# One-bank operations for the channel mix, the DFT pair and the output projection of a gated recurrence with long convolution

## The chip, the cores and the metric

The kernel runs on one core of a Trainium2 chip. The metric is the device time of one execution in microseconds. The engines are TensorE (PE, with its weight loads shown apart as PEld), VectorE (DVE), ScalarE (ACT), GpSimd (POOL) and SyncE (SP), which issues the DMAs. PE writes only to PSUM, which has eight banks of 512 f32 values per partition; ACT and DVE carry results out of it ("evictions").

## The reference

Batch B = 4, sequence S = 6272 = 128 x 49, D = 256 channels.

```python
sig = 1.0 / (1.0 + np.exp(-f_logit))
f = lower_bound + (1.0 - lower_bound) * sig
i = 1.0 - f
for t in range(S):                 # the recurrence
    h = f[:, t] * h + i[:, t] * x[:, t]
    y[:, t] = h
...
proj = y @ w_proj                  # [B, S, 3 D] -> x1, x2, x3
X2 = np.fft.rfft(x2, n=S, axis=1)
H = np.fft.rfft(filter_fft, n=S, axis=0)
x2_conv = np.fft.irfft(X2 * H, n=S, axis=1)
out = (x1 * x2_conv * x3) @ w_out
```

## The kernel before, in words

The kernel works through the four batches, with the recurrence of the next batch spread over the current one. The transform of length 6272 is split as 128 (m) times 49 (q).

- **Recurrence** (`hgrn`): PE turns chunks of x and f_logit (`su`, line 374, f32, two row tiles of 64 rows), ACT or DVE makes the gate (`f`, lines 387 and 389), DVE scans (line 395) and writes the states as f16 into `HA`, channels on partitions, time along the row.
- **P** (`phase_p`, line 720), the channel mix to x2: for each of the 49 residues r, the stationary operand is a column of HA, every 49th element (`column`, line 716), and the moving one is `W2`, 256 columns; two matmuls (one for each half kh of the states' channels) accumulate. Four r fill two banks. The eviction `x2` (line 732) writes f16 into X2, one run of four for each output channel. P reads all states of the batch.
- **F1** (`phase_f1`, line 737), the DFT over m: eight matmuls of 128 columns for a unit of eight channel pairs, two banks, evicted as `A` (line 745). 16 units a batch, four at a time.
- **F2** (line 804), the DFT over q, two banks, then the product with the filter's spectrum: directly by DVE from PSUM (line 827), or by a copy to A and POOL (line 836).
- **I2** (line 842), the inverse over q: both halves o of the product, 16 matmuls of 98 columns into two banks, evicted as `Th` (line 851).
- **Gate** (`gate`): x1 and x3 by matmuls x13 (line 423, one bank each); their product z goes to `zt` (line 444 by DVE, line 453 by POOL).
- **Output** (`phase_o`, line 896): I1 (line 909), the inverse over m; DVE multiplies by z into `ys` (line 915, f32r, two buffers); proj (line 927) multiplies by w_out into two banks, evicted as `o` into a staging place, and SP stores it.

The copies carry the line of the helper `copy`: 289 and 291 for ACT, 294 and 296 for DVE. So a group is told by its output tile: X is x2, HA 128x1024 is A, HA 98x512 is the copy ahead of POOL's product, Th, osb or PP is o.

Nothing is scheduled at run time. Each step is declared with `op(kind, cost, fn, r, w, take, src)`: what it reads and writes as tokens, how many banks it takes, and for an eviction the operation that it empties. The text `ORDER` (line 126) then lists all operations in the order in which they are emitted. Three characters in base 64 hold one of them: its index, its engine, and its first bank (`Plan.order`, line 100). So the order on each engine, the engine of each eviction and every bank are written out. An operation of PE is of one of two kinds: those that use tiles of 64 rows (`ROWS`, line 65: su, F2, mini, I1, FF2, last) and those that use all rows.

```python
word = a * 4096 + b * 64 + c
yield word // 64, self.ENGINES[word // 8 % 8], word % 8
```

At the start the filter is transformed (f2, FF1, FF2), its spectrum is written to DRAM, and each unit loads its part again (`Hu`). `pads` zeroes the gaps of X2 between the runs.

Of the kernel before, what the change touches and what calls it, by code (L numbers as in the profile page):

```python
# [25 lines left out]
Q = 49  # L26
# [27 lines left out]
def q_of(r):  # L54

    return (18 * r) % Q
# [6 lines left out]
class Plan:  # L63
# [63 lines left out]
    "AAYAPYA0gA4gA5YACIADIAQIAWIA1AAiQAdQA8gAkQAbQBAgBIgAcQAeQAgQA2QAhSAfSA9YA6SApUAjUA+UAmWBEgBQgBMgBBYATYAzIARAASAA7CA3"  # L127
    "IAUIBCWA/MBFIBDGAsQAoQAtQBJYBKQAxSAlSBGSArWAXABHKBYgDogBUgBggBcgBkgDrgDpgDsgEDgDqgD3gAnWAZWBRABSUBZAAaOAEgD4gEbgEEgB"
    "NYBOSAvWBLAEPgEQgAYYBVYBTMBPKABIAqWBaWAyUBbGBWUBdIBhYAuSBiSBjKBeWBlYBXEBfGDtAAwQBmQEFAAVYBnIBoWBpOBqQBrIBsYBxSBvWByK"
    "BwODuYBtQBuIB4SB6WD5AB5KB7OB0UB1EAFYBzYB8YD6YDvQCBSCCCDzUDwIDxID0EB/WCAGCDYEGYD1MCKSB9QCLKCEWD7UCFOEdAB+AD8ECISCJCCR"  # L130
    "QD/WCPSERACSACQCD9MCNUEHQCOECUSEAOEBOCYWEcgEzgEngEogEIIEJIE0gELUE9gCVCCMYCTYESYCZGE1ACaSCbCCfWCgGEMMENMChQCiIETSEpAE"
    "eYCcYCjYEqYCdWEXUCeGCoQEYEEUKEVKCkWEZMCpAClGEfSE/ACvQCqUEjWEgKCwIEhKCrEEkGCxQErUCyIElOCtSFHgAGgFJAEvQEsEEtME+gCWgFIg"
    "FRgCuCAHgFSgFbgC4WEwAExIEKYE2YCsYAIYAJYAKYCzYE3SFAYC6UC5GE4CC7EFKYC8YAMYC0WE5KE6QC1GC/UE7IDBSFTADAMDCCE8IFBWC9UFESFC"
    "GC+EFDOFFCCHgFcgFlgB3gFmgFvgFwgDIQDJADKUDLEDEWDFGALIEWYAOYDDYDMYFUYDyYFLQFOUFGKFPEDPSFMIFNIDQCFdAFQMDaWDNSDOCDbGFeYA"
    "NYFVQFYUFZEFnAFWIFXIDRSJSWJTXFfQJUGDSCJVHFxAFaMJXWFiSFgIJZOFhIFjCDUUDVEFkKFoYFpWDhQEmYDTYEiYEuYFyYD2YEOYECYEaYD+YFsU"
    "DfSFqGFrODiADYQFtEDgCDZAFuMFzWDkSF0GF2QEyADdUCGgB2gC3gDeEDlCC2gMXgDHgG2gCXgMWgF5gCmgMigDXgCngF+gDcYDjYJWYMYAF6YF7YMZ"
    "YGkgDmgMvgDngMjgDGgDWgMugGtgG/gF1OJYWJcXF3IJeHF4IGMQGCUGISGJCJauGNIGDMGQQGGWGHOGUSGYUGVKGRAGOQGKWGPIMkAGZEGLGGEUGFEG"
    "ASGSWGWUGBKGTGJdSJhTJiWJfqGXEGaUGbEJjLJkuGcQGdAGgSGhKGeWJmUJnVGfGF8QJoMJpNGlSGuWGiUF9AGpqGyGG3QGjMJrXJsTG5AGnqGwuJbY"
    "GqYJqYJtHHIUJwXJxQGxYGmYJuDGzYGoYGvYJyHJzoGrSG7oHJEHAWG0UGsCG1EHOSHPCJ1RJ2QHKUHEuG4YJvYG6YG8YHBYMlYHFYJ3JHCuHLEJ6XHM"
    "SJ7RJ8PJ4oJ9pHNCG9UHTWG+EHSgHDYHQSJ/QHGUKARHbgHkgHtgHXGKBAHRKMwAHVuKCpHcSHHEHlWHnGKERHeqHgqH2UHWYHdYKFWKJSKGBHfYHUYH"  # L140
# [24 lines left out]
    "kUXFAXGIXSQafCXaSdeAXbCUlMUqOXgUXYWXMSXhEXTIXWUXNKXXMXZGXOWXPGdqAUmSXiUUnKXUWXeQXQSXVOXfIXjEd2AXKWXRCXLGXcUXdEUogUjg"
    "UzSUuQdfYUrWUvIU0KdrYXIYXJYd3YUsGXmUacYXnMXoQXkSXqWXpAXrGaeUUwQagEXlKXsWXtOUxAXuSdgUXwqXyCX2WdhEaiQajTanSaoRX6uakAX4"
    "GahYXxYalrapCdkWaqBXvYX3YXzYX5YX7YdlGasQdiMX0SauAdmOYOUX+QYCIYAoX1CYPEdsSYGWdtCYIGX8UYKuX/YYBYarYatRaxWayQavpYLYYDYY"
    "YgeAgYJYeBgYqgYhgX9EYSUduKazGa0AYEWYZQYdoYTEYFGYQUYREa2SYUWa3Ta7Ra4Ka5rYeYYboY8UYHYa1YYcYYVGYWSYXKdwWa9BY9EeCAa8RbAQ"
    "bBSbDCbCAYMUYiSdxOa+pdyOYmqYNEYkCYaYYnYbEYa/YYlYYjYd4QbFWd5AbHGd6Id8Ud9Ed+MYfSYrWYgCYtGY+QYoSY0UY/AYzgUtgZGgeMgeYgZP"
    "gYvuY4sY2sY5YYsYYuYY3YeDYY1YYwYYpCZCQZDAeZgZYgZhgeNgZAWbGSbKTbIqZBGbMDYxQZEWZHUYyAZFOZLsZQSY6WZUqZJEbLUeEQbNsZSCY7GZ"  # L170
    "ZWeFAZIYZKYZMYeISZdGeGIeJCZNUZbueKKbPXZVYZOEZTYZRYZiQbRHZsUZWWZkoZmAbQRbUSZeYZcYZtEZXGeOAZnYZaYbWKbSpZuUZlYZqWZvEZrG"
    "bVQbZSbaTbeRbXoZwUbbKbgJbcrbfSU1WZfQZxEU2ObhqZyWZ1UZjYePYZzOeQSeaAZ0gZ9gekgelgaGgZgAaPgU3gdbgeugfDge4gfCgZ5EZ3sebYbY"
    "YbJYZoWeRKeSKZ+QZpGaCAbOYZ2YZ4YZ6YaDYZ/Ya6YeUUaHWeVEbjRecSeWMaJGaLGblBedCbkWboXaAoZ7UaBYbmubqHbpRbtXbuQbyWbrpeeKZ8Eb"
    "zRb3UbvHb0Gbwob1paQWegSb4Qb8Rb5Mb6oemAaUGehCaEUeiKewAb+BaFEb9QcBXcCRb/oaSucDHcEpaTYaIYaKYenYbdYaMYaRYamYbnYcFYb2YaVY"
    "eoSerUcGXcHWepCesEcIHeqKaNQcJuaOAcLXcMScQTetMcNHcOqaWQcSDaXAcRXcVTcWWcTvcXDcfQcAYcUYi7XcaSfXgevgfgge5gUyge6Ai9HdnYcK"
    "YbxYexYb7YbiYcPYcYucZYd/YbsYeXYdjYbTYe7YeyUe1WezEe2GejYawYcgIchQcbKccSe0MckUciAcdCfMgfWgfNgcegcjge3Oe8QcpWcuSclMcmUc"
    "qOe9AfEAcrWcnEcsGe+IczQe/UcvKc0Ic4ScwWfAEfOAcxGc1Qc2AfBMc5Kc9UeTYfFYfGWfPYfJSfQQc+MfHGfKCfYAfIOc6Uc/WfLKfRAc7EfSIdCS"
    "fTUdAGdDKfUEfVMi8QjARi+AjCBdHWdIOfqgcygfhgfZYefYctgcogc3gdvYfrYd7YfaSfdQfbCfeAfiAdEUdFEdJWdKGfcKffIc8gdGgdLgeLYfjYfs"
    "YdzYfkSfnUdRQeHYdMWflKfmKfoEfpMgFUgGEdSIdNOf9Sf3Qf7Uf4Af8EfzWftQf1UfuIf+CgDSf0Gf2EgECf5Qf/UgAEgBSgCKf6IfxWfyGfvUfwEd"
    "OSdWQdPCgHUjBWdXIjDugIEi/YgNQgLSgOAgJWgMKgRUjFQjGRgKGgVsgPWgZSgQOgTsgdqjHAjIBdQgg7ggbCgUYgaYgWYgSYgeYjKVjMFdYQgxWgyG"  # L180
    "gXUghWglugcYjJYgmYgjugkYgiYgYEdZAgpSgzUgfQgrCgtqg0EjLXjPSggAg1Ug3QjQWjRCjSujNvg2EgnSg8UhAsgsYg4AhFQg5Wg6Og+sgoChHAhE"
# [12 lines left out]
def kernel(  # L194
# [135 lines left out]
    def lend():  # L330

        op("pre", {"SP": 0.01}, lambda e: None, w=x2t)
# [680 lines left out]
```

## Time and profile before

| what | value |
|---|---|
| median of 3 runs | 454.33 us (454.22 to 454.91) |
| the profiled execution | 453.94 us |
| its span in the trace | 452.2 us |
| granted PE clock over the span | 0.997 |
| HBM read, written | 86.12 MB, 31.98 MB |
| DMA queue of the kernel's transfers | 118.11 MB, 71.9% of 16 engines' span |
| chain that ended last | PE 74%, DVE 13%, DMA 4%, issue 3%, ACT 3% |

The span is that of the trace from its first to its last instruction; the rest of the execution, 1.74 us, lies around it. A busy share counts an instruction from its start to its end, and matmuls are pipelined, so that PE's busy time is no proof that it is at its peak. The time from one matmul's start to the next says more, and the chain of waits gives it where it lists many in a row. A group's row gives line, engine, operation, output and inputs, shape and count, then busy us and the mean ns of one, then the idle time before and what ended it.

### The profile page before, as it was taken

To read this page: it belongs to the slowest core of one execution; us is meant where nothing else is said; L and a number is where in the kernel's file an instruction comes from. 1 tells how busy PE (TensorE), PEld (TensorE's weight loads), DVE (VectorE), ACT (ScalarE), POOL (GpSimd) and SP (SyncE) were. 2 spreads that over 40 slices of the span, in tenths; PEclk is the share of its full clock that TensorE was granted. 3 is DMA by queue.
4 is the path that set the end of the run, shared out by engine and by line. 5 is a ranking of instruction groups with operands and counts; after the bars stand their busy time and mean duration, and the time that the engine had idled before them with its cause. 6 is when DMAs were issued, how large, how long until landed. Compare 5 with 4: busy or idle time off the path is not lost.

```text
span 452.2 us, 14532 instructions
## 1 busy us (share of the span) xinstructions
PE 436.2 (96%) x6013; PEld 345.1 (76%) x6013; DVE 407.1 (90%) x459; ACT 391.1 (86%) x539; POOL 317.6 (70%) x301
## 2 busy tenths in 40 slices
PE   8899999999999999999999999999999999999994
PEld 7787768777667889767768989777769897766783
DVE  8799998799999997999999987999999948989774
ACT  6679999899999968999999869999988979987553
POOL 6578998289999942678997828969996805676400
PEclk9999999999999999999999999999999999999998
DMA  8999999657998475777966992598946613763167
GB/s 330 407 368 334 404 368 367 253 187 249 371 356 308 191 230 229 240 255 244 410 249 189 323 319 106 199 327 307 386 161 236 269 71 107 225 235 102 49 268 304
DMA packets 42563, 119.05 MB, mean 263 GB/s; under 512 B 4096, under 2 KB 5760, under 8 KB 42496
## 3 DMA queue, kind: packets, MB, share of 16 engines
q1 hardware_dynamic: 42496, 118.11, 71.9%
q8 instruction: 47, 0.77, 0.7%
q14 instruction: 20, 0.16, 0.1%
HBM read 86.12 MB, written 31.98 MB: 261 GB/s over the span
## 4 chain that ended last, share of the span: by engine, by line
PE 74%; DVE 13%; DMA 4%; issue 3%; ACT 3%; POOL 1%; SPq 0%; DVEq 0%; ACTq 0%; POOLq 0%
PE PS L423 18%; PE PS L846 10%; PE PS L729 10%; PE PS L927 7%; PE PS L374 7%; PE PS L804 7%; DVE HA L395 7%; PE PS L742 6%; DVE ys L915 4%; PE PS L909 3%; PE PS L666 3%; DMA HA<-in_moe_filter_fft_dram 3%; DMA X<-in_moe_filter_fft_dram 1%; PE PS L684 1%; POOL PP L836 1%
## 5 line engine op out<-in xcount | busy, mean ns | idle before, releaser
L395 DVE TENSOR_TENSOR_SCAN HA<-fTs,HA,PS 128x512 f16<-128x512 f32 (+1 forms) x96 | 112.5, 1201 | 1.3 <-ACT fTs L387 0.6
L423 PE MATMUL PS<-HA,W 128*128 128x490 f16 (+1 forms) x416 | 102.1, 367 | 0.1
L836 POOL TENSOR_TENSOR PP<-HA,Hu 98x1008 f16<-98x1008 f16 x46 | 96.4, 2104 | 4.8 <-ACT HA L289 2.8
L289 ACT CAST HA<-PS 128x1024 f16<-128x1024 f32 (+1 forms) x107 | 85.0, 824 | 4.4 <-PE PS L742 2.4
L362 POOL TENSOR_TENSOR XT<-XT,FL 128x1024 f32<-128x1024 f32 (+1 forms) x31 | 67.0, 2165 | 20.1 <-ACT FL L360 20.0
L915 DVE TENSOR_TENSOR ys<-PS,zt 128x1024 fp32r<-128x1024 f32 (+1 forms) x52 | 58.4, 1152 | 10.4 <-PE PS L909 6.9
L387 ACT ACTIVATE fTs<-PS,nomc 128x512 f32<-128x512 f32 (+1 forms) x88 | 57.9, 669 | 7.2 <-PE PS L374 2.0
L927 PE MATMUL PS<-Wo,ys 128*128 128x256 f32 x392 | 57.6, 293 | 3.7 <-DVE ys L915 2.8
L444 DVE TENSOR_TENSOR zt<-PS,XS 128x490 f16<-128x490 f32 (+1 forms) x88 | 55.9, 649 | 5.6 <-PE PS L423 3.4
L827 DVE TENSOR_TENSOR PP<-PS,Hu 98x1008 f16<-98x1008 f32 x50 | 59.0, 1198 | 1.2 <-PE PS L804 0.7
L846 PEld LDWEIGHTS <-PP 98*128 98x128 f16 x1024 | 49.7, 97 | 11.2 <-POOL PP L809 2.0
L362 POOL TENSOR_TENSOR X<-X 128x1024 f32<-128x1024 f32 x21 | 50.0, 2382 | 9.6 <-ACT X L360 7.4
L846 PE MATMUL PS<-FT,PP 98*128 98x98 f16 x1024 | 55.7, 206 | 0.4 <-POOL PP L809 0.2
L927 PEld LDWEIGHTS PS<-Wo,ys 128*128 128x128 f32 x392 | 49.4, 188 | 8.4 <-DVE ys L915 2.6
L423 PEld LDWEIGHTS <-W 128*128 128x128 f16 x416 | 34.7, 97 | 27.7 <-issue 3.6
L289 ACT CAST Th<-PS 128x784 f16<-128x784 f32 x61 | 49.8, 819 | 5.6 <-PE PS L846 4.8
L291 ACT ACTIVATE XS<-PS 128x490 f32<-128x490 f32 (+1 forms) x84 | 48.5, 579 | 4.1 <-PE PS L423 1.9
L729 PE MATMUL PS<-W,HA 128*128 128x256 f16 x392 | 43.8, 273 | 0.1
L729 PEld LDWEIGHTS <-HA 128*128 128x128 f16 x392 | 42.9, 142 | 0.5
L809 POOL TENSOR_TENSOR PP<-zp 98x32 f16<-98x32 f16 x64 | 19.3, 339 | 31.1 <-DVE zp L763 26.9
L289 ACT CAST X<-PS 128x1024 f16<-128x1024 f32 (+1 forms) x32 | 31.8, 1054 | 10.1 <-PE PS L729 9.7
L804 PE MATMUL PS<-HA,FT 64*128 64x256 f16 x512 | 38.0, 271 | 0.5 <-ACT Hm L291 0.2
(113 smaller groups left out, 772.7 us busy)
## 6 DMA issues: line engine op xcount, KB each, us to landing
Hu<-H SPq DMA_DIRECT2D x39, 512.0 KB, 4.8
FL<-in_f_logit_dram SPq DMA_DIRECT2D x27, 512.0 KB, 6.0
XT<-in_x_dram SPq DMA_DIRECT2D x27, 512.0 KB, 6.7
out_dram<-osb SPq DMA_DIRECT2D x24, 512.0 KB, 5.3
X<-in_f_logit_dram SPq DMA_DIRECT2D x21, 512.0 KB, 7.6
X<-in_x_dram SPq DMA_DIRECT2D x21, 512.0 KB, 8.2
out_dram<-PP SPq DMA_DIRECT2D x16, 512.0 KB, 4.5
Hl<-H SPq DMA_DIRECT2D x13, 512.0 KB, 4.6
```

The costliest lines, as they stand in the source:

```text
L289: nc.scalar.copy(dst, src)
L362: op("u", {"POOL": 0.1 + 0.553 * nb}, lambda e, xt=xt, ft=ft: nc.gpsimd.tensor_tensor(xt, xt, ft, op=AOP.mult), r=[("ft", k)], w=[("xt", k)])
L387: nc.scalar.activation(fT, sT, AF.Identity, scale=by, bias=1.0)
L395: nc.vector.tensor_tensor_scan(h, fT, bank(pb)[:, 512 - hn:512 + hn], init, op0=AOP.mult, op1=AOP.add),
L423: nc.tensor.matmul(PS[:, p, 0:n], W13[:, kh, js], HA[:, HB[kh] + t0:HB[kh] + t0 + n], start=(kh == 0), stop=(kh == 1))
L729: nc.tensor.matmul(pp[:, r - r0, :], column(HB[kh], q_of(r)), W2[:, kh, :], start=(kh == 0), stop=(kh == 1))
L804: nc.tensor.matmul(PS[:, xb + e2, :].rearrange("p (i k) -> p i k", k=64)[:, :, ks], FT(rows, o, r), A[rows, ka:ka + UE, r, ks], start=(r = ...
L827: nc.vector.tensor_tensor(pr, px.unsqueeze(1).broadcast_to([TB, 2, UE, 63]), hh(), op=AOP.mult)
L836: nc.gpsimd.tensor_tensor(pr, spec[:, o, :, 1:64].unsqueeze(1).broadcast_to([TB, 2, UE, 63]), hh(), op=AOP.mult)
L846: nc.tensor.matmul(PS[:, ib + o, pr * TB:(pr + 1) * TB], PP[:TB, k, o, n, 2 * pr:2 * pr + 2, :], v[:TB], start=(n == 0), stop=(n == 1))
L915: nc.vector.tensor_tensor(late["ys"][:, yk, :, 0:rn * 128], PS[:, cb:cb + 2, 0:rn * 128], late["zt"][:].rearrange("p k r m -> p k (r m)") ...
L927: nc.tensor.matmul(po[:, i, :], late["ys"][:, yk, kh, i * 128:(i + 1) * 128], Wo[:, kh, :], start=(kh == 0), stop=(kh == 1))
```

## The change

P, F1, I2 and proj each take one bank at a time where they took two, so each becomes two operations with two evictions:

- P runs over the output channels by halves h: for each group of four r and each h, matmuls of 128 columns; the order of the halves alternates with the batch, as that of the units does. The pads, and the tokens of X2, are split by halves too.
- F1 does four channel pairs in one operation; it reads only the half of X2 that its unit lies in (unit 7 reads both).
- I2 is one operation for each o.
- proj is one operation for each two r, its eviction `o` also; a store still carries four r.
- The declared costs follow. `ORDER` is another text: 2893 operations in place of 2430, and with it the sequence on every engine, the banks, and the engine of each eviction.

```diff
 ORDER = (
...
 )
     def At(u):
-        return [("At", u % NA)]
+        return [("At", u % NA, o) for o in range(2)]
     def Ax(u):
     more_t = [[("raw", 2 * j), ("raw", 2 * j + 1)] for j in range(3)]
     slots0 = (0, 1, 2, 3, 4, 5, 0, 1, 2, 3, 4, 0, 1)
     count["x"] = 2
-    x2t = [("raw", i) for i in range(7)] + [("x2", g) for g in range(NX2)] + ["padX"]
-    x2t += [(t, NX + i) for t in ("ft", "xt") for i in range(3)]
+    x2t = [[("raw", 3 * h + i) for i in range(4)] + [("x2", g, h) for g in range(NX2)] + [("padX", h)]
+           + [(t, NX + h + i) for i in range(2) for t in ("ft", "xt")] for h in range(2)]
     def lend():
-        op("pre", {"SP": 0.01}, lambda e: None, w=x2t)
+        for h in range(2):
+            op("pre", {"SP": 0.01}, lambda e: None, w=x2t[h])
     def pads():
-        op("pad", {"POOL": 2.0}, lambda e: nc.gpsimd.memset(xv[:, :, Q:64], 0.0), w=["padX"])
-
-        def tails(e):
-            nc.gpsimd.memset(xv[:, :, 113:PW], 0.0)
-            nc.gpsimd.memset(X2[:, NEP * PW:], 0.0)
-        op("pad", {"POOL": 0.6}, tails, w=["padX"])
+        for h in range(2):
+
+            def gaps(e, h=h):
+                rows = slice(h * NEP // 2, (h + 1) * NEP // 2)
+                nc.gpsimd.memset(xv[:, rows, Q:64], 0.0)
+                nc.gpsimd.memset(xv[:, rows, 113:PW], 0.0)
+                if h:
+                    nc.gpsimd.memset(X2[:, NEP * PW:], 0.0)
+            op("pad", {"POOL": 1.36}, gaps, w=[("padX", h)])
     def hgrn(b):
         for c in range(NCHK):
     def phase_p(b):
         hn = [("hn", kh, c) for kh in range(2) for c in range(NCHK)]
-        for g, r0 in enumerate(range(0, Q, 4)):
-            rn = min(4, Q - r0)
-
-            def mm(e, pb, r0=r0, rn=rn):
-                pp = PS[:, pb:pb + 2].rearrange("m a (r e) -> m (a r) e", e=256)
-                for r in range(r0, r0 + rn):
-                    for kh in range(2):
-                        nc.tensor.matmul(pp[:, r - r0, :], column(HB[kh], q_of(r)), W2[:, kh, :],
-                                         start=(kh == 0), stop=(kh == 1))
-            pp = op("P", {"PE": 0.005 + 0.214 * rn}, mm, r=hn + Wr(0) + Wr(1) + ["W2"], take=2)
-            op("x2", either(256 * rn), lambda e, pb, r0=r0, rn=rn: copy(
-                e, both(xv[:, :, r0:r0 + rn]),
-                PS[:, pb:pb + 2].rearrange("m a (r e) -> m (a r) e", e=256)[:, 0:rn, :]
-                .rearrange("m r (i e) -> m i e r", e=2)), w=[("x2", g)], src=pp)
+        for h in range(2) if b % 2 == 0 else (1, 0):
+            for g, r0 in enumerate(range(0, Q, 4)):
+                rn = min(4, Q - r0)
+
+                def mm(e, pb, r0=r0, rn=rn, h=h):
+                    for i in range(rn):
+                        for kh in range(2):
+                            nc.tensor.matmul(PS[:, pb, i * 128:i * 128 + 128], column(HB[kh], q_of(r0 + i)),
+                                             W2[:, kh, h * 128:h * 128 + 128], start=(kh == 0), stop=(kh == 1))
+                pp = op("P", {"PE": 0.113 * rn}, mm, r=hn + Wr(0) + Wr(1) + ["W2"], take=1)
+                op("x2", either(128 * rn), lambda e, pb, r0=r0, rn=rn, h=h: copy(
+                    e, both(xv[:, h * 64:h * 64 + 64, r0:r0 + rn]),
+                    PS[:, pb, 0:rn * 128].rearrange("m (r i e) -> m i e r", r=rn, e=2)),
+                   w=[("x2", g, h)], src=pp)
     def phase_f1(b, u):
-        def mm(e, pb):
-            pa = PS[:, pb:pb + 2].rearrange("m a (i c) -> m (a i) c", c=128)
-            for i in range(UE):
-                j = (u * UE + i) * PW
-                nc.tensor.matmul(pa[:, i, :], X2[:, j:j + 128], D1, start=True, stop=True)
-        f1 = op("F1", {"PE": 0.056 * UE}, mm, r=[("x2", g) for g in range(NX2)] + ["D1", "padX"], take=2)
-        k = u % NA * UE
-        op("A", either(1024), lambda e, pb: copy(
-            e, A[:, k:k + UE],
-            PS[:, pb:pb + 2].rearrange("p a (i r k) -> p (a i) r k", r=2, k=64)),
-           w=At(u) + Ax(u), src=f1)
+        for h in range(2):
+            hn = UE // 2
+
+            def mm(e, pb, h=h):
+                for i in range(hn):
+                    j = (u * UE + h * hn + i) * PW
+                    nc.tensor.matmul(PS[:, pb, i * 128:i * 128 + 128], X2[:, j:j + 128], D1, start=True, stop=True)
+            f1 = op("F1", {"PE": 0.056 * hn}, mm, r=[t for i in ((0, 1) if u == NU // 2 - 1 else (u * 2 // NU,))
+                                                 for t in [("x2", g, i) for g in range(NX2)] + [("padX", i)]] + ["D1"],
+                    take=1)
+            k = u % NA * UE + h * hn
+            op("A", either(512), lambda e, pb, k=k: copy(
+                e, A[:, k:k + hn],
+                PS[:, pb].rearrange("p (i r k) -> p i r k", r=2, k=64)),
+               w=[At(u)[h], Ax(u)[h]], src=f1)
     def mini(b, q):
         n = NA * UE
             op("pm", {"POOL": 2.27}, late_prod,
                r=() if direct else [("Hu", h), ("Ax", u % NA, o)], w=[("P", k, o)])
-        def inv(e, ib):
-            for o in range(2):
+        for o in range(2):
+
+            def inv(e, ib, o=o):
                 for pr in range(UE // 2):
                     for n, v in enumerate((VA, VB)):
-                        nc.tensor.matmul(PS[:, ib + o, pr * TB:(pr + 1) * TB],
+                        nc.tensor.matmul(PS[:, ib, pr * TB:(pr + 1) * TB],
                                          PP[:TB, k, o, n, 2 * pr:2 * pr + 2, :], v[:TB],
                                          start=(n == 0), stop=(n == 1))
-        i2 = op("I2", {"PE": 0.695}, inv,
-                r=[("P", k, 0), ("P", k, 1), ("Pz", k, 0), ("Pz", k, 1), "VA", "VB"], take=2)
-        op("Th", either(784), lambda e, ib: copy(
-            e, late["Th"][:, :, u // 8, :, u % 8 * 4:u % 8 * 4 + 4],
-            PS[:, ib:ib + 2, 0:392].rearrange("p a (g c) -> p c a g", g=4)),
-           r=["cz"], w=[("Th", u)], src=i2)
+            i2 = op("I2", {"PE": 0.35}, inv, r=[("P", k, o), ("Pz", k, o), "VA", "VB"], take=1)
+            op("Th", either(392), lambda e, ib, o=o: copy(
+                e, late["Th"][:, :, u // 8, o, u % 8 * 4:u % 8 * 4 + 4],
+                PS[:, ib, 0:392].rearrange("p (g c) -> p c g", g=4)),
+               r=["cz"], w=[("Th", u, o)], src=i2)
     def spectrum(b):
         phase_p(b)
             return v[:, 0:rn], a[:, 0:rn]
         return v, a.rearrange("p (j r) e -> p j r e", j=2)
-    def place_t(kind, i):
-
-        return {"p": lambda: [(t, i, o) for t in ("P", "Pz") for o in range(2)],
-                "a": lambda: [t for j in (2 * i, 2 * i + 1) for t in At(j) + Ax(j)],
-                "z": lambda: [("zr", i)], "o": lambda: [("osb", i)]}[kind]()
+    def place_t(kind, i, h):
+
+        return {"p": lambda: [(t, i, h) for t in ("P", "Pz")],
+                "a": lambda: At(2 * i + h) + Ax(2 * i + h),
+                "z": lambda: [("zr", i, h)], "o": lambda: [("osb", i, h)]}[kind]()
     places = (("o", 0), ("o", 1), ("p", 0), ("p", 1), ("a", 0), ("a", 1), ("o", 0),
                   ("o", 1), ("p", 0), ("p", 1), ("o", 0), ("o", 1), ("o", 0))
                             nc.tensor.matmul(PS[:, cb + p, i * 128:(i + 1) * 128],
                                              tf[ps, c0:c0 + 128], ID[ps, rr, sh:sh + 128],
                                              start=(rr == 0), stop=(rr == 1))
-            i1 = op("I1", {"PE": 0.115 * rn}, inv, r=[("Th", u) for u in range(NU)] + ["ID"], take=2)
+            i1 = op("I1", {"PE": 0.115 * rn}, inv, r=[("Th", u, o) for u in range(NU) for o in range(2)] + ["ID"], take=2)
             yk = g % 2
             op("y", {"DVE": 0.05 + rn * 0.267}, lambda e, cb, yk=yk, r0=r0, rn=rn:
                nc.vector.tensor_tensor(
                r=["cv"] + [("z", jb, c) for jb in range(2) for c in range(NCHK)],
                w=[("y", yk)], src=i1)
-            def proj(e, ob, yk=yk, rn=rn):
-                po = PS[:, ob:ob + 2].rearrange("m a (r e) -> m (a r) e", e=256)
-                for i in range(rn):
-                    for kh in range(2):
-                        nc.tensor.matmul(po[:, i, :], late["ys"][:, yk, kh, i * 128:(i + 1) * 128],
-                                         Wo[:, kh, :],
-                                         start=(kh == 0), stop=(kh == 1))
-            po = op("proj", {"PE": 0.259 * rn}, proj, r=[("y", yk)], take=2)
-            at, kt = places[g], place_t(*places[g])
-
-            def stage(e, ob, at=at, rn=rn):
-                to, of = rows_of(*at, PS[:, ob:ob + 2].rearrange("m a (r e) -> m (a r) e", e=256), rn)
-                copy(e, to, of, OS)
+            at = places[g]
+            kt = place_t(*at, 0) + (place_t(*at, 1) if rn > 2 else [])
+            for j in range(0, rn, 2):
+                jn = min(2, rn - j)
+
+                def proj(e, ob, yk=yk, j=j, jn=jn):
+                    for i in range(jn):
+                        for kh in range(2):
+                            nc.tensor.matmul(PS[:, ob, i * 256:i * 256 + 256],
+                                             late["ys"][:, yk, kh, (j + i) * 128:(j + i + 1) * 128],
+                                             Wo[:, kh, :], start=(kh == 0), stop=(kh == 1))
+                po = op("proj", {"PE": 0.259 * jn}, proj, r=[("y", yk)], take=1)
+
+                def stage(e, ob, at=at, rn=rn, j=j, jn=jn):
+                    v = place(*at)
+                    to = v[:, j // 2] if at[0] == "z" else v[:, j:j + jn]
+                    copy(e, to, PS[:, ob, 0:jn * 256].rearrange("m (r e) -> m r e", e=256), OS)
+                op("o", either(256 * jn), stage, w=place_t(*at, j // 2), src=po)
             def leave(e, at=at, r0=r0, rn=rn):
                 of, to = rows_of(*at, out[b].rearrange("(a r) d -> a r d", r=Q)[:, r0:r0 + rn, :], rn)
                 nc.sync.dma_start(to, of)
-            op("o", either(256 * rn), stage, w=kt, src=po)
             op("store", {"SP": 0.46}, leave,
                r=kt, w=[t for t in kt if t[0] == "zr"], dma=0.37 * rn, lag=1.3, margin=MARGIN)
```

More of the change, by code (lines that the diff above doesn't have):

```diff
@@ L131 @@
[L131 to L140, printed above, removed]
```

128 lines of the change are left out of this document (75 added, 53 removed).

## The prediction

> **What bounds the kernel now.** I read the page first, then the busy time by stage, then the chain of waits, then the groups by line and shape, and last the list of who waited for whom.
>
> ```profile
> span 452.2 us, 14532 instructions
> PE 436.2 (96%) x6013; PEld 345.1 (76%) x6013; DVE 407.1 (90%) x459; ACT 391.1 (86%) x539; POOL 317.6 (70%) x301
> ```
>
> PE, DVE and ACT are all nearly full on average, so the stages have to be told apart. In the table of windows the columns are the window, its length, and the busy time of PE, PEld (weight loads), DVE, ACT and POOL, then clock, DMA share and GB/s. These are mixing stages (F1, F2, products, I2, with the gate's x13), output stages that share the time with the next batch's recurrence, and the tail:
>
> ```profile
> 82.30:139.00 56.70, 55.89 (x828) 39.83 (x828) 55.05 (x64) 54.25 (x80) 48.22 (x40) 1.00 0.80 280
> 139.00:165.80 26.80, 25.91 (x456) 21.96 (x451) 26.57 (x27) 24.31 (x35) 23.22 (x22) 1.00 0.62 225
> 176.70:236.00 59.30, 59.24 (x857) 43.21 (x857) 57.22 (x67) 56.00 (x83) 45.97 (x37) 1.00 0.76 270
> 275.80:340.00 64.20, 64.13 (x959) 47.05 (x959) 60.99 (x71) 60.93 (x92) 58.00 (x50) 1.00 0.68 244
> 340.00:362.30 22.30, 21.68 (x378) 18.98 (x378) 22.21 (x23) 19.65 (x26) 16.42 (x16) 1.00 0.70 266
> 373.20:425.00 51.80, 51.52 (x657) 36.85 (x657) 45.18 (x59) 44.41 (x65) 34.23 (x32) 1.00 0.44 146
> 425.00:452.20 27.20, 20.29 (x294) 17.77 (x288) 16.93 (x16) 11.73 (x12) 0.28 (x1) 0.94 0.65 257
> ```
>
> Mixing is bound by PE (55.89 of 56.70, 59.24 of 59.30), with DVE and ACT close behind. In the output stages it is DVE that is full (26.57 of 26.80, 22.21 of 22.30). Between the two lies phase P, the channel mix that the change cuts in halves:
>
> ```profile
> 71.57:82.27 10.70, 10.70 (x99) 10.62 (x98) 7.36 (x7) 9.40 (x11) 5.50 (x5) 1.00 1.00 368
> 165.83:176.68 10.85, 10.85 (x101) 10.85 (x101) 8.88 (x8) 7.56 (x9) 2.38 (x1) 1.00 0.82 296
> 263.93:275.83 11.90, 11.90 (x110) 11.69 (x110) 9.43 (x8) 9.19 (x10) 5.93 (x3) 1.00 0.84 308
> 362.36:373.24 10.88, 10.88 (x100) 10.88 (x101) 5.06 (x5) 8.77 (x9) 0.00 (x0) 1.00 0.13 50
> sum 44.33, PE 44.33 PEld 44.04 DVE 30.72 ACT 34.92 POOL 13.81; mean PE 11.08 PEld 11.01 DVE 7.68 ACT 8.73 POOL 3.45
> ```
>
> Here PE has no idle time at all, and DVE has 44.33 - 30.72 = 13.6 us of it. The chain of waits (start, length, what) runs through P without a break, and gives the pace of the other matmuls:
>
> ```profile
> 71.57 10.70 PE PS L729 x98
> 142.96 1.00 PE PS L374 x32
> 270.20 0.94 PE PS L927 x8
> 277.64 1.80 PE PS L742 x32
> 362.36 10.88 PE PS L729 x98
> ```
>
> A P matmul (256 columns) takes 10.70/98 = 109 ns, an F1 matmul (L742, 128 columns) 1.80/32 = 56 ns, a proj matmul (L927, f32, 256 columns) 0.94/8 = 118 ns. The transposes of L374 run as pairs on two row tiles: 1.00/16 = 62.5 ns for a pair.
>
> **P: twice the matmuls, twice the weight loads.** Per column of q there were two matmuls of 256 columns; now there are four of 128, and each loads its column of HA again: 392 pairs of load and matmul become 784. If a matmul of 128 columns paced them, as in F1, P would cost 784 x 56.25 ns = 44.1 us against 392 x 109.2 = 42.8: +1.3. But the weights of P are not those of F1. They are every 49th element of HA, and the groups of weight loads (shape, count, busy us, mean ns of one) show it:
>
> ```profile
> L927 PEld LDWEIGHTS PS<-Wo,ys 128*128 128x128 f32 x392 | 49.4, 188 | 8.4 <-DVE ys L915 2.6 <-issue 1.3 <-DVE HA L395 1.2
> L729 PEld LDWEIGHTS <-HA 128*128 128x128 f16 x392 | 42.9, 142 | 0.5
> L742 PEld LDWEIGHTS <-X 128*128 128x128 f16 x512 | 31.1, 98 | 9.2 <-issue 3.1 <-ACT X L289 0.2
> L374 PEld LDWEIGHTS PS<-idc,X 64*128 64x128 f32 x672 | 23.8, 139 | 6.0 <-DVE HA L395 3.3 <-ACT XS L291 0.4 <-ACT afs L289 0.4
> ```
>
> The same 128x128 f16 takes 98 ns from X and 142 ns from HA. Only part of a load stands in the way of the next matmul, as F1 shows (98 ns of load in a 56 ns pace). How much, the loads of nearly the same length say: L374 loads in 139 ns, its matmuls have only 64 columns, and a pair goes out every 62.5 ns, so 76 ns of the load are hidden. By that row P's pace is 142 - 76 = about 65 ns. By L927 (188 ns in a pace of 118, 70 hidden) it is 72 ns. Today's 109 ns hides either. The ends are 56 ns (+1.3 us) and 72 ns (784 x 72 = 56.4, +13.6); I take 65, the row nearest in load time: 51.0 us, **+8.2 us**, in stages where PE has no idle time to hide it.
>
> [...]
>
> **Starting F1 before P ends.** F1 of units 0 to 6 now needs one half of x2 only (unit 7 reads into both, so it waits for all). That would remove a PE wait for evictions of x2, but there is hardly one:
>
> ```profile
> PEld L742 <- ACT X L289: 0.2, 1, 0.2
> PEld PS L374 <- ACT HA L289: 1.6, 4, 0.4
> PEld PS L374 <- ACT Th L289: 0.9, 3, 0.4
> PEld L804 <- issue: 4.4, 12, 0.4
> PEld L423 <- issue: 3.6, 17, 0.4
> ```
>
> F1 waited 0.2 us for x2 in the whole run; proj, x13 and I1 fill PE there. Worth 0 to PE. Decoding the new order, batch 0 issues 24 of its 26 P operations before the first F1 anyway; batch 3 spreads them furthest, past the first I2.
>
> **More, smaller evictions.** F1, I2, P and proj each give up one bank at a time. The order decoded gives, before to after, on ACT: A 58 to 106, Th 61 to 113, x2 32 to 59, o 48 to 90, prod 49 to 56; on DVE: A 6 to 22, Th 3 to 15, x2 20 to 45, o 4 to 10, direct products 74 to 68, xs copies 23 to 17.
>
> ```profile
> L827 DVE TENSOR_TENSOR PP<-PS,Hu 98x1008 f16<-98x1008 f32 x50 | 59.0, 1198 | 1.2 <-PE PS L804 0.7 <-ACT XS L291 0.2 <-ACT HA L289 0.2
> L289 ACT CAST HA<-PS 128x1024 f16<-128x1024 f32 x58 | 57.4, 1022 | 3.2 <-PE PS L742 2.4
> L289 ACT CAST HA<-PS 98x512 f16<-98x512 f32 x49 | 28.3, 590 | 1.2 <-PE PS L804 0.9
> L296 DVE TENSOR_SCALAR XS<-PS 128x490 f32<-128x490 f32 x19 | 12.4, 660 | 0.2
> L294 DVE CAST HA<-PS 128x1024 f16<-128x1024 f32 x6 | 7.2, 1220 | 0.6 <-PE PS L742 0.5
> L294 DVE CAST HA<-PS 98x512 f16<-98x512 f32 x5 | 3.4, 689 | 0.8 <-PE PS L804 0.7
> ```
>
> Two halves are 2 x 590 - 1022 = 158 ns longer than a whole on ACT, and 2 x 689 - 1220 = 158 on DVE. But queued instructions overlap: in the timeline (start, length) the next one starts before the last has ended.
>
> ```profile
> 421.48 0.81 ACT L289 CAST Th<-PS 128x784 f16<-128x784 f32 x1
> 422.18 0.60 ACT L291 ACTIVATE XS<-PS 128x490 f32<-128x490 f32 x1
> ```
>
> The second starts 0.70 us after the first, so 0.11 us of each instruction is free when there is a backlog, and a split costs 158 - 110 = about 48 ns. With that, the counts add some 1 us on ACT (the growth went to DVE) and some 9 us on DVE: A +6, Th +4, x2 +4, o +3, less 6.5 for six direct products and 3 for six copies, plus 3 for five more x3 products. The 4 of x2 fall in P, where DVE idles 13.6 us. The other 5 fall in stages where DVE is full or nearly so: 0 if PE covers them, +5 if all shows, and I take **+1.5**.
>
> **Shorter holds of the banks.** A half is held about half as long, so PE waits less for evictions. Of the waits listed, 1.6 (A, before su) and 0.9 (Th, before su) are of this kind. In the tail, which has no other batch's work to fill it, these are PE's waits:
>
> ```profile
> PEld PS L927 <- DVE ys L915: 1.9, 2, 1.6
> PEld PS L927 <- ACT HA L291: 0.6, 1, 0.6
> PE PS L927 <- DVE ys L915: 2.8, 4, 1.4
> ```
>
> y itself is not split, so of the 4.7 us that proj waits for it I count 1, and the whole 0.6. That makes 1.6 + 0.9 + 0.6 + 1 = about **-4**. The ends are 0, because a new order makes waits elsewhere, and -10: PE is idle 6.9 us in the tail and less than 1 us in each mixing stage.
>
> **The order itself.** PE's sequence changes between operations on 64 rows and on 128 rows 230 times before and 216 times after. The waits called "issue" before L804 (0.37 us each) and L423 (0.21) stand at such changes: 14 fewer is 0 to -3, I take **-1**. The prologue has the same work in another sequence: 0, give or take 2. The memsets of the pads are the same elements on POOL, idle in P. More P and proj instructions bring no more DMA; the stores keep their size.
>
> **Sum.** The profiled execution took 453.94 us, its span of 452.2 and 1.74 around it; it lies 0.39 below the median of 454.33. 453.94 + 8.2 + 1.5 - 4 - 1 = **458.6 us**, 1% slower.
>
> **Rivals.**
> (1) P stays paced by its matmuls at 56 ns: 453.94 + 1.3 + 1.5 - 4 - 1 = 451.7. For it: today's 109 ns stream never shows a bare load, and F1 hides a 98 ns load fully. Against: L374's pace with loads of the same length. [...] Chance 0.15.
> (2) DVE takes work forward. The finer P leaves banks free for products and y within P, and half of DVE's 13.6 us of idle time there is taken out of the output stages, where DVE is the bound: 458.6 - 6.8 = 451.8. It decides if DVE's busy share in the P stretches rises from 69% to over 85%. For it: batch 3 mixes P with F2 and I2. Against: PE has to feed that work in a stage in which it is full. Chance 0.15.
> (3) Nothing is recovered and the smaller evictions show: 453.94 + 8.2 + 5 - 1 = 466.1. For it: DVE's 26.57 of 26.80. Chance 0.15. [...]
> (4) The halves change nothing that can be told: gains and losses cancel to 454.3. Chance 0.1.
>
> **How the numbers follow.** The forecast, 455.3 to 463, has 0.45. Slower by over 0.2% (about what this measurement can tell from no change) are it and (3): 0.60; within 0.2%, 0.10; faster, (1) and (2), 0.30. The range 451 to 465 leaves out the lower edge of (1) and (2) and the far part of (3).
>
> **What would show it.** The gap between P's matmuls: 62 to 68 ns bears the main term out, 56 brings down the sum by 7. P's total of weight loads, with P's stretch (first to last, less what is mixed in) 12 to 13.5 us a batch. The wait of F1 for x2 stays near zero. ACT's busy time for A about as before, DVE's up. The tail's proj waits for ys drop by about a microsecond. The prediction is wrong if P's pace is right but the mixing or output stages shrink by more than 5 us together, which would say that bank holds, not PE's stream, set their length.

## The result, and the profile after

The changed kernel takes 460.0 us (median, 458.91 to 461.23) against 454.36 before: a ratio of 1.0121, interval 1.0108 to 1.0135, 5.6 us slower. The forecast was 458.6. The six executions fall into two groups, three at 458.91 to 459.04 us and three at 460.96 to 461.23, so that the median lies where none of them does, and differences of a microsecond to this kernel are uncertain. The profiled execution, of 461.08 us, is one of the upper group. Part of its time lies at its start: the first P matmul begins at 73.6 us, while with the same prologue in run 1 below it begins at 70.8; between 20 and 30 us the granted clock is 0.83 here and 1.00 in the kernel before, and run 1 has 0.999 over its whole span. In what follows, single executions far from all others (1035 us in run 3, 682 us in run 8, whose trace is therefore not read) are left out of the medians and ratios.

The page of the kernel after, its span and busy times:

```profile
span 459.3 us, 15595 instructions
...
PE 443.7 (97%) x6405; PEld 355.3 (77%) x6405; DVE 418.2 (91%) x521; ACT 394.6 (86%) x715; POOL 320.9 (70%) x300
```

PE has 392 more matmuls and 7.5 us more busy time; ACT has 176 more instructions and 3.5 us more, DVE 62 and 11.1 us. PE's idle time hardly moves: 452.2 - 436.2 = 16.0 us before, 459.3 - 443.7 = 15.6 us after. So the longer span is PE's longer work. The chain of waits of the kernel after (start, length, what), where it runs through P:

```profile
73.59 10.52 PE PS L745 x164
...
370.01 9.67 PE PS L745 x148
```

10.52/164 = 64 ns and 9.67/148 = 65 ns from one P matmul to the next. The groups by line and shape show the loads and the evictions:

```profile
L301 ACT CAST HA<-PS 128x512 f16<-128x512 f32 x106 | 59.1, 608 | 3.7 <-PE PS L760 3.0 <-POOL PP L829 0.2 <-PE PS L824 0.2
...
L301 ACT CAST Th<-PS 128x392 f16<-128x392 f32 x113 | 53.6, 511 | 2.4 <-PE PS L867 2.2
...
L745 PEld LDWEIGHTS <-HA 128*128 128x128 f16 x784 | 53.1, 152 | 1.9 <-issue 0.2
```

A load of P's weights now takes 152 ns; in the slower stream before it took 142. The table of windows, cut at P (window, length, then busy PE, PEld, DVE, ACT, POOL), of the kernel before and of the kernel after:

```profile
82.10:165.80 83.70, 81.99 (x1279) 61.89 (x1276) 81.62 (x90) 78.76 (x114) 71.44 (x60) 1.00 0.74 262
165.80:176.50 10.70, 10.70 (x101) 10.70 (x99) 8.73 (x8) 7.41 (x9) 2.38 (x1) 1.00 0.83 301
...
sum 380.70, PE 369.84 PEld 292.18 DVE 342.02 ACT 330.63 POOL 260.11; mean PE 46.23 PEld 36.52 DVE 42.75 ACT 41.33 POOL 32.51
```

```profile
73.45:89.50 16.05, 16.05 (x237) 15.21 (x235) 12.76 (x21) 12.75 (x22) 7.80 (x10) 1.00 0.96 353
89.50:169.45 79.95, 78.45 (x1239) 59.98 (x1238) 79.01 (x89) 74.89 (x142) 68.75 (x59) 1.00 0.74 259
169.45:188.60 19.15, 19.15 (x281) 18.57 (x280) 15.43 (x21) 15.62 (x28) 8.52 (x7) 1.00 0.60 230
...
270.05:291.70 21.65, 21.65 (x304) 19.99 (x302) 18.25 (x27) 15.95 (x30) 11.22 (x8) 1.00 0.46 168
...
369.95:390.60 20.65, 20.65 (x320) 19.62 (x317) 18.28 (x26) 14.09 (x28) 4.95 (x6) 1.00 0.44 165
...
sum 385.85, PE 376.50 PEld 301.50 DVE 356.71 ACT 330.84 POOL 267.22; mean PE 47.06 PEld 37.69 DVE 44.59 ACT 41.35 POOL 33.40
```

The P stretch of batch 1 grew from 10.70 to 19.15 us, because F1 and parts of the output are mixed into it, and the stretch ahead of it fell from 83.70 to 79.95. PE is busy without a gap in P as before, in all four batches (19.15 of 19.15 us in batch 1). From the first P to the end the kernel needs 385.85 us in place of 380.70.

### The profile page after: what moved, and what is told of

Same layout as the page of the kernel before. It is cut to its first block, busy times and chain, and to the rows that moved or that the text cites. A ratio compares the mean times of both kernels' runs of the same rounds, so it can differ in the third digit from the quotient of the medians.

```text
span 459.3 us, 15595 instructions
## 1 busy us (share of the span) xinstructions
PE 443.7 (97%) x6405; PEld 355.3 (77%) x6405; DVE 418.2 (91%) x521; ACT 394.6 (86%) x715; POOL 320.9 (70%) x300
## 4 chain that ended last, share of the span: by engine, by line
PE 74%; DVE 15%; DMA 4%; issue 3%; ACT 2%; POOL 1%; SPq 0%; DVEq 0%; ACTq 0%; POOLq 0%
PE PS L439 17%; PE PS L745 11%; PE PS L867 10%; PE PS L951 10%; DVE HA L411 8%; PE PS L390 7%; PE PS L824 6%; PE PS L760 6%; PE PS L929 4%; DMA HA<-in_moe_filter_fft_dram 2%; DVE ys L935 2%; PE PS L682 1%; DMA X<-in_moe_filter_fft_dram 1%; DVE fTs L405 1%; DVE afs L306 1%
## 5 line engine op out<-in xcount | busy, mean ns | idle before, releaser
L856 POOL TENSOR_TENSOR PP<-HA,Hu 98x1008 f16<-98x1008 f16 x51 | 107.1, 2108 | 6.7 <-ACT HA L301 4.6
L301 ACT CAST HA<-PS 128x512 f16<-128x512 f32 (+1 forms) x162 | 89.9, 605 | 7.2 <-PE PS L824 3.2
L460 DVE TENSOR_TENSOR zt<-PS,XS 128x490 f16<-128x490 f32 (+1 forms) x93 | 59.5, 651 | 3.4 <-ACT XS L303 1.1
L867 PE MATMUL PS<-FT,PP 98*128 98x98 f16 x1024 | 61.5, 206 | 0.2
L301 ACT CAST Th<-PS 128x392 f16<-128x392 f32 x113 | 53.6, 511 | 2.4 <-PE PS L867 2.2
L745 PE MATMUL PS<-W,HA 128*128 128x128 f16 x784 | 55.4, 228 | 0.0
L745 PEld LDWEIGHTS <-HA 128*128 128x128 f16 x784 | 53.1, 152 | 1.9 <-issue 0.2
L847 DVE TENSOR_TENSOR PP<-PS,Hu 98x1008 f16<-98x1008 f32 x45 | 53.3, 1197 | 0.2
L301 ACT CAST X<-PS 128x512 f16<-128x512 f32 (+1 forms) x59 | 33.6, 604 | 16.4 <-PE PS L745 15.9
L760 PE MATMUL PS<-D,X 128*128 128x128 f16 x512 | 41.3, 219 | 0.0
```

Source lines behind the costliest of these rows:

```text
L301: nc.scalar.copy(dst, src)
L460: nc.vector.tensor_tensor(zd(), px, xs(0), op=AOP.mult)
L745: nc.tensor.matmul(PS[:, pb, i * 128:i * 128 + 128], column(HB[kh], q_of(r0 + i)), W2[:, kh, h * 128:h * 128 + 128], start=(kh == 0), stop ...
L760: nc.tensor.matmul(PS[:, pb, i * 128:i * 128 + 128], X2[:, j:j + 128], D1, start=True, stop=True)
L856: nc.gpsimd.tensor_tensor(pr, spec[:, o, :, 1:64].unsqueeze(1).broadcast_to([TB, 2, UE, 63]), hh(), op=AOP.mult)
L867: nc.tensor.matmul(PS[:, ib, pr * TB:(pr + 1) * TB], PP[:TB, k, o, n, 2 * pr:2 * pr + 2, :], v[:TB], start=(n == 0), stop=(n == 1))
```

## The experiments

A run's ratio is against the kernel before on the same chip, with its 95% interval.

**1. The loads of P from adjacent elements, in the changed kernel.**

```diff
     def column(t, q):
-        n0 = t + 128 * q - (S // 2 if q > Q // 2 else 0)
-        return HA[:, n0:n0 + Q * 127 + 1:Q]
+        return HA[:, t + S - 128:t + S]
```

> The changed kernel, with P's stationary operand read from 128 adjacent elements of the last chunk of HA instead of every 49th element (the output is no longer the reference's; the same number of loads and matmuls, and P still waits for the last scan). Theory (the step of the weight loads paces the halved matmuls): weight loads near 98 ns, P's pace 56 ns in place of 65, 784 x 9 = 7.3 us less: 452.7 us, below the kernel before. Rival (the loss comes from the new order and the smaller evictions): P's pace may change, the time stays within 1.5 us of 460.

Measured: 452.0 us, ratio 0.9958 (0.9942 to 0.9974). The group of P's loads and the chain of this run:

```profile
L744 PEld LDWEIGHTS <-HA 128*128 128x128 f16 x784 | 44.8, 98 | 2.3 <-issue 0.2
```

```profile
70.80 9.16 PE PS L744 x164
```

The load takes 98 ns and the pace is 9.16/164 = 56 ns. Nothing else in the kernel changed, and the medians differ by 8.0 us. The traces say where: from the first P matmul to the end it is 459.3 - 73.6 = 385.7 us against 449.7 - 70.8 = 378.9, 6.8 us less, and the other 2.8 us between the two profiles lie ahead of P, where the kernels are the same. So the step of the loads is worth about 7 us here. With P paced by its matmuls the change would have been a gain: the theory holds and the rival falls.

**2. and 3. Only the split of P's matmuls, in the kernel before.** The order, the banks and the evictions stay:

```diff
-                    for kh in range(2):
-                        nc.tensor.matmul(pp[:, r - r0, :], column(HB[kh], q_of(r)), W2[:, kh, :],
-                                         start=(kh == 0), stop=(kh == 1))
+                    for h in range(2):
+                        for kh in range(2):
+                            nc.tensor.matmul(pp[:, r - r0, h * 128:h * 128 + 128], column(HB[kh], q_of(r)),
+                                             W2[:, kh, h * 128:h * 128 + 128], start=(kh == 0), stop=(kh == 1))
```

The third run has the `column` of the first run besides.

> The kernel before, its order and banks untouched, with each P matmul of 256 columns issued as two of 128 with their own weight loads. Theory: P's pace 65 ns per matmul, +8.4 us, all of it on the path: 462.8 us. Rival (loads stay hidden, pace 56): +1.0, 455.4 us.

> The same split of P's matmuls in the kernel before, with the stationary operand from adjacent elements (the output is no longer the reference's). Theory (the step is the cause): pace 56 ns, 455.4 us. Rival (twice as many loads and instructions cost this, whatever they read): about 462.

Measured: 462.06 us, ratio 1.0169 (1.0155 to 1.0183), with the step; 455.26 us, ratio 1.0013 (1.0003 to 1.0023), without it. These are P's pieces in the chains: in the kernel before, batches 1 and 2 (batches 0 and 3 have 10.70 and 10.88 us for 98 matmuls each); then all four batches with the step; then the first batch without it:

```profile
165.83 10.85 PE PS L729 x98
...
263.93 6.26 PE PS L729 x56
271.14 4.69 PE PS L729 x42
```

```profile
71.87 12.76 PE PS L730 x196
...
168.16 12.74 PE PS L730 x196
...
268.32 7.37 PE PS L730 x112
276.69 5.48 PE PS L730 x84
...
368.71 12.86 PE PS L730 x196
```

```profile
72.00 10.94 PE PS L729 x196
```

12.76/196 = 65 ns and 10.94/196 = 56 ns. All of P takes 51.2 us with the step against 43.4 before, 7.8 us more, and the kernel takes 7.7 us more. The split alone costs 7.7 us with the step, and 0.9 us with the same number of loads, matmuls and instructions but adjacent elements. So it is the step of the loads, and not their number, that costs 6.8 of the 7.7 us. One rival is left, since runs 1 and 3 also read the same 128 elements each time. Run 11 below does so too, at a step of 16, and is slow, which rules it out.

**4. and 5. P whole again in the changed kernel.** P and x2 go back to the form before; F1, I2, proj and their evictions stay as changed. In run 4 the 13 P of a batch take every second place of the 26; whatever depends on them is put off. In run 5 they all stand ahead of the batch's first F1.

```diff
-        for h in range(2) if b % 2 == 0 else (1, 0):
-            for g, r0 in enumerate(range(0, Q, 4)):
...
+        for g, r0 in enumerate(range(0, Q, 4)):
...
+                .rearrange("m r (i e) -> m i e r", e=2)), w=[("x2", g, h) for h in range(2)], src=pp)
```

> The changed kernel with P and its eviction x2 as before (two banks, matmuls of 256 columns, evictions of 1024); F1, I2 and proj stay one-bank operations, and the new order is kept as far as P allows it (F1 waits for all of P, P's banks chosen anew). Theory (the change lost P's 8.4 us and its other parts are about even): 451.6 us, between 450.5 and 453.5. Rival (the halves paid for part of their cost by letting F1, DVE and ACT start early): 455 or more.

> As the run before with P as two-bank operations of 256 columns, but the order is kept much closer: the 13 P of a batch stand in the places that P had ahead of the batch's first F1, so that nothing behind them is put off (four banks moved, no operation by more than 12 places). Theory (without P's 8 us the rest of the change gains some 3): 450.5 to 452.5 us. Rival (the early start of F1 by halves is what gains): 454 or more. If the 485.8 us of the first try come from P as such and not from its displaced order, this run shows them too.

Measured: 485.82 us, ratio 1.0708 (1.0683 to 1.0732), and 473.62 us, ratio 1.0427 (1.0407 to 1.0447). Both theories are far off. In the waits of the second of them, F1 (L757) stands out:

```profile
PEld L757 <- issue: 10.1, 18, 2.4
...
PE PS L757 <- ACT X L298: 3.7, 2, 2.2
```

and its chain at the end of P of batch 1 is a row of engines that wait for each other:

```profile
179.60 1.02 ACT X L298
180.62 0.04 issue
180.66 0.63 PE PS L926 x16
181.29 1.04 PE PS L742 x8
182.33 0.02 issue
182.35 0.04 DVE X L303
182.39 1.10 issue
183.49 1.22 DVE ys L932
184.72 0.04 issue
184.76 0.40 PE PS L757 x4
```

The wait of F1's loads called "issue" is 10.1 us here; in the changed kernel it is 1.3. The likely reading is this: the new order has F1 right behind P, and relies on the first half's evictions being done while P's second half runs. With P whole, F1 waits for the last x2, where the old order has proj and x13. So the two runs do not price P; they show that these two ways of putting a whole P into the new order do not work. The listed waits of F1 are not all of the loss: the mixing stages of these runs are longer too, and why was not settled. In run 4 the granted clock is lower besides, 0.977 over the span against 0.995 in run 5.

**6. The other three phases in one-bank operations, in the old order.** Each F1, I2 and proj of the old order is replaced in place by its halves, on the same two banks; P and x2 stay as they were.

```diff
-        f1 = op("F1", {"PE": 0.056 * UE}, mm, ..., take=2)
+            f1 = op("F1", {"PE": 0.056 * hn}, mm, ..., take=1)
...
-        i2 = op("I2", {"PE": 0.695}, inv, ..., take=2)
+            i2 = op("I2", {"PE": 0.35}, inv, ..., take=1)
...
-            po = op("proj", {"PE": 0.259 * rn}, proj, r=[("y", yk)], take=2)
+                po = op("proj", {"PE": 0.259 * jn}, proj, r=[("y", yk)], take=1)
```

> F1, I2 and proj as one-bank operations with their evictions, P and x2 as before, everything in the order of the kernel before (each former operation replaced by its two halves, in place, on the same banks). Theory (shorter holds gain by themselves): 451 to 453 us. Rival (the gain lies in the new order; alone, the smaller evictions only cost): 454.5 to 457.

Measured: 452.77 us, ratio 0.9965 (0.9951 to 0.9978). This version beats both kernels: -1.7 us against the one before, -7.2 against the changed one. The finer operations of F1, I2 and proj gain by themselves. But the waits that I had counted for them are hardly smaller in the list of this run:

```profile
PEld PS L387 <- ACT HA L298: 1.3, 3, 0.5
...
PEld PS L387 <- ACT Th L298: 0.8, 2, 0.4
...
PEld PS L948 <- ACT HA L300: 0.6, 1, 0.6
```

1.3 in place of 1.6, 0.8 of 0.9, 0.6 of 0.6.

**7. Only the evictions split.** In the kernel before, each x2, A, Th and o is issued as two instructions, one for each half, on the same engine; for A:

```diff
-        op("A", either(1024), lambda e, pb: copy(
-            e, A[:, k:k + UE],
-            PS[:, pb:pb + 2].rearrange("p a (i r k) -> p (a i) r k", r=2, k=64)),
+        op("A", either(1024), lambda e, pb: [copy(
+            e, A[:, k + 4 * h:k + 4 * h + 4],
+            PS[:, pb + h].rearrange("p (i r k) -> p i r k", r=2, k=64)) for h in range(2)],
```

> The kernel before with each eviction of x2, A, Th and o issued as two instructions on the same engine, nothing else changed: 199 more instructions on ACT, 29 on DVE. Theory (48 ns each, mostly beside PE's work): 454.4 to 456.5 us, ACT's busy share up. Rival (DVE and ACT have no room, all of it shows): 199 x 0.048 = +9.5, about 463.

Measured: 454.21 us, ratio 0.9996 (0.9987 to 1.0005): no difference. The page:

```profile
span 451.9 us, 14787 instructions
...
PE 437.3 (97%) x6013; PEld 345.6 (76%) x6013; DVE 409.0 (91%) x490; ACT 398.5 (88%) x736; POOL 317.3 (70%) x301
```

ACT's busy time rises by 398.5 - 391.1 = 7.4 us for 197 more instructions, 38 ns each, and the kernel is no longer for it. DVE has only 31 more instructions here and 409.0 - 407.1 = 1.9 us, so this run says little of the 11.1 us by which DVE grew in the changed kernel.

**8. All one-bank operations in the old order.** As run 6, with P and x2 in channel halves as in the change; each former operation is replaced in place by its parts.

> All one-bank operations of the change, P in halves among them, but in the order of the kernel before (each former operation replaced in place by its parts; F1 still comes behind all of P). Theory (P's halves +7.6 and the finer F1, I2, proj -1.7, as the runs so far gave; the new order and the early start of F1 are worth little): 460.3 us, 459 to 461.5. Rival (the new order is worth several us): 463 or more.

Measured: 460.70 us, ratio 1.0137 (1.0119 to 1.0155). The new order with the early F1 makes 460.0 of that. It is worth 0.7 us by the medians, which cannot be told from nothing: the intervals of the two ratios overlap.

**9. proj alone.** As run 6, with F1 and I2 left as before.

> The kernel before with proj and its eviction o alone as one-bank operations, in place in the old order. Theory (the 1.7 us come from the tail and the output stages, where proj waits): 453.0 us. Rival (they come from F1 and I2 in the mixing stages): 454.2.

Measured: 453.52 us, ratio 0.9985 (0.9975 to 0.9994), 0.8 us of the 1.7. Between the two expectations: the output gives about half; the other half is left for F1 and I2, which were not run alone.

**10. and 11. Other steps of the load.** The kernel of run 2 with `HA[:, n0:n0 + k * 127 + 1:k]` that ends with the last state, for k = 2 and 16; one execution each.

> P's matmuls in halves in the kernel before, the stationary operand read at a step of 2 elements (the output is no longer the reference's). If any step above 1 costs the same: weight loads 142 ns, 462 us. If the cost grows with the bytes skipped: between 98 and 142 ns, 455.3 to 462.

> The same at a step of 16 elements (the output is no longer the reference's). Any step the same: 142 ns and 462 us. A load that depends on how the elements fall on lines or banks of memory: another value than at steps 2 and 49.

Measured: 455.36 us at step 2, 460.29 us at step 16. The groups of P's loads, first step 2, then step 16, then step 49 (run 2):

```profile
L730 PEld LDWEIGHTS <-HA 128*128 128x128 f16 x784 | 44.0, 98 | 0.6
```

```profile
L730 PEld LDWEIGHTS <-HA 128*128 128x128 f16 x784 | 49.4, 148 | 0.5
```

```profile
L730 PEld LDWEIGHTS <-HA 128*128 128x128 f16 x784 | 51.3, 153 | 0.5
```

Every second element loaded as fast as adjacent ones, in 98 ns; at step 16 the load took 148 ns, nearly as long as the 153 at 49. The chain at step 16 has P's pace, 12.21/196 = 62 ns:

```profile
71.79 12.21 PE PS L730 x196
```

**12. P in one-bank operations by rows.** As run 8, but an operation of P does two rows r with all 256 columns, so that the loads stay 392; an eviction then writes runs of two.

```diff
-                for i in range(rn):
-                    for kh in range(2):
-                        nc.tensor.matmul(PS[:, pb, i * 128:i * 128 + 128], column(HB[kh], q_of(r0 + i)),
-                                         W2[:, kh, h * 128:h * 128 + 128], start=(kh == 0), stop=(kh == 1))
+                for i in range(rn):
+                    for kh in range(2):
+                        nc.tensor.matmul(PS[:, pb, i * 256:i * 256 + 256], column(HB[kh], q_of(r0 + i)),
+                                         W2[:, kh, :], start=(kh == 0), stop=(kh == 1))
```

> All four phases as one-bank operations in the order of the kernel before, but P by pairs of rows r (256 columns each, 392 loads as before) instead of by channel halves; an eviction x2 then writes runs of two f16 in place of four. Theory (the halved columns are what cost; the loads are hidden again): P's pace 109 ns; 452.8 us if an eviction of 512 in runs of two takes some 0.6 us. Rival (short runs are slow: the x2 of 256 elements in runs of one took 1.33 us in the kernel before): evictions of 1.2 us, 26 a batch on two engines against 10.7 us of P, 15.6 - 10.7 = 5 us a batch, 465 or more.

Measured: 453.85 us, ratio 0.9989 (0.9979 to 0.9998). From the chain and the groups of this run:

```profile
71.82 10.70 PE PS L743 x98
```

```profile
L300 ACT CAST X<-PS 128x512 f16<-128x512 f32 x58 | 32.8, 717 | 4.7 <-PE PS L743 4.7
...
L305 DVE CAST X<-PS 128x512 f16<-128x512 f32 x38 | 23.7, 686 | 9.4 <-PE PS L743 9.1 <-DMA FL<-in_f_logit_dram 0.2
```

P is back at 109 ns. The rival's slow short runs do not show: an eviction takes 0.69 to 0.72 us, not 1.2. Against run 8, which differs in the way P is cut and nothing else, this is 6.9 us less. The same one-bank P costs 7 us more if it is cut by columns than if it is cut by rows. Cut by rows it still gains nothing: run 6, with P whole, has 452.77 us.

## Why the prediction was right

It was right in sign and size (458.6 for 460.0), by the mechanism that it named. By its terms:

- **P, +8.2 taken, 7.7 measured alone** (run 2). That the step of the loads sets P's pace is shown: 56 ns at step 1 (at step 2 the loads' busy time is 44.0 us, as in run 3), 62 at 16, 65 at 49. The pace of 65 ns that was forecast came out at 64 to 65, but the way to it is not borne out. It took a load of 142 ns and left out the 76 ns that L374's pairs hide. In the halved P the load itself reads 152 to 153 ns, and 87 to 88 of them are hidden; at step 16 it is 148 - 62 = 86. With the load as it came, the same subtraction would have given 76 ns and +16.8 us. The two errors cancel, and the closeness of the 65 is luck to that extent. Of the two ends, 56 and 72 ns, run 3 gives the lower one itself, at 56 ns and +0.9 us where +1.3 was worked out.
- **Cover.** The term was put on the path whole, because PE has no gap in P. Run 2 confirms it: 7.8 us more in P's chain are 7.7 us more in the kernel.
- **Early F1, 0 taken, and the order, -1 taken.** The new order with the early start is worth 0.7 us (run 8 against the changed kernel), which fits both but is not told from nothing. How much of it is the order's and how much the early start's was not told apart.
- **Smaller evictions, +1.5 taken, none measured where they were tested** (run 7: -0.2 us, interval -0.6 to +0.2). The price of one, 48 ns, was near the 38 ns measured on ACT. But the term was about DVE, and run 7 adds little there. The items that the prediction lists for DVE add up to 10.5 us, not to 9; 11.1 were measured. What that growth costs is part of what the new order gives in sum, and was not tested by itself.
- **Shorter holds, -4 taken, -1.7 measured** (run 6), the term most mis-sized. I had added up waits that the list names, as if each would vanish. In run 6 they are almost all still there, and the gain came in small pieces, about half of it in the output. In the changed kernel the wait for A before su is no longer listed, but others are. In its tail, proj's waits for ys fall from 4.7 to 3.6 us, the microsecond that was forecast, and its wait for an eviction grows from 0.6 to 1.3 us:

```profile
PEld PS L951 <- DVE ys L935: 1.4, 2, 0.9
PEld PS L951 <- ACT PP L303: 1.3, 1, 1.3
...
PE PS L951 <- DVE ys L935: 2.2, 3, 1.2
```

- **The sum.** 7.7 - 1.7 - 0.7 = 5.3 of the 5.6 us, from terms that are each known to about half a microsecond or worse. That the forecast lies 1.4 us from the result is partly luck: the two mis-sized terms, 1.5 too much cost and 2.3 too much gain, nearly cancel.

Of the rivals, (1) failed on P's pace, but run 1 is what it described, 452.0 us for the 451.7 worked out. (2) had asked for DVE to be busy over 85% of the P stretches, from 69%. It came close: 64.72 of 77.50 us in the four stretches, 84%, and by batch 80, 81, 84 and 89%. But the stretches are longer because work of other stages is mixed into them, and the new order that does this is worth 0.7 us, not 6.8. (3) needed evictions that show and nothing recovered; run 7 saw no cost for more evictions on ACT, and run 6 recovered 1.7 us. (4) falls with the measured interval, 4.9 to 6.1 us slower.

## What to carry to other kernels

Splitting an operation by the moving columns repeats its weight loads (784 for 392 here); before that, compare the group's mean load with that of a group whose weights lie adjacent (here 142 against 98 ns). A longer load is a warning that it may show once the matmuls are shorter (here 65 ns for a matmul of 128 columns against 56 with adjacent weights); how much has to be measured, by halving the matmuls alone as run 2 does. A one-bank operation that covers whole columns of fewer rows gets the shorter hold without the second load (392 loads in run 12): the same four phases took 453.85 us cut by rows and 460.70 cut by columns. And an order written out for one set of operations prices nothing when one of them is changed back under it: P made whole again in the new order cost 14 to 26 us more than the changed kernel.

## What the runs showed of the hardware that had not been expected

- A 128x128 f16 weight load of P took 98 ns at a step of 1 (runs 1 and 3) and at a step of 2 (run 10), 148 ns at 16 (run 11) and 152 to 153 at 49 (the kernel after and run 2).
- The same load at step 49 read 142 ns in the kernel before and in run 12, at a pace of 109 ns with matmuls of 256 columns, and 152 to 153 ns in the kernel after and in run 2, at a pace of 64 to 65 with matmuls of 128. So the duration that the profile gives this load was not the same in the two streams; which of their differences made it longer was not tested.
- An ACT eviction of x2, 512 elements to f16, took 717 ns with runs of two and 596 (the kernel after) to 622 (run 7) with runs of four, while DVE took 686 with runs of two and 692 (the kernel after) with runs of four. So from four to two only ACT took longer here, by 15 to 20%. With runs of one both were slow: in the kernel before, the x2 of 256 elements took 1333 ns on ACT and 1324 on DVE. The rows for runs of two stand at run 12; those for runs of four are from the kernel after, and the last from run 7:

```profile
L301 ACT CAST X<-PS 128x512 f16<-128x512 f32 x56 | 31.4, 596 | 16.4 <-PE PS L745 15.9 <-issue 0.2
...
L306 DVE CAST X<-PS 128x512 f16<-128x512 f32 x40 | 26.6, 692 | 7.5 <-PE PS L745 5.4 <-ACT X L301 1.1 <-ACT XS L303 0.9
```

```profile
L289 ACT CAST X<-PS 128x512 f16<-128x512 f32 x58 | 29.7, 622 | 8.0 <-PE PS L729 7.5 <-DVE ys L915 0.4
```
